# Float32 value products in the sixth to eighth pair of heads, in place of VectorE's low halves

## Chip, cores and metric

The kernel runs on one core of a Trainium2 chip. The metric is the device time of one launch in microseconds (us), the median over several runs. One execution of the same program was recorded by the hardware profiler; every row below is from that execution.

## What is computed

Attention with pooled queries, then a gated feed-forward block, then a soft mixture of experts. Only the attention is touched by the change:

```
q_pool = q.reshape(B, H, S // 2, 2, D).mean(axis=3)          # B=4, H=8, S=1152, D=64
scores = (1 / sqrt(D)) * matmul(q_pool, k.transpose(0, 1, 3, 2))
scores = scores - max(scores, axis=-1)
attn   = exp(scores) / (sum(exp(scores)) + 1e-9)
x      = matmul(attn, v)                                     # -> (2304, 512)
h      = silu(x @ w_gate) * (x @ w_val)                      # d_ff = 1536
y      = h @ w_out ; then dispatch, 8 experts (512 -> 1024 -> 512), combine
```

All inputs and the output are float32.

## The kernel before

**Steps and units.** The attention walks over 16 steps, one for each batch and pair of heads (`steps`, four pairs in each of four batches). A step has 21 units: nine key chunks of 128 for each of the two heads against 512 queries, and three units that hold the remaining 64 queries of both heads (six 64-wide parts each). `unit` computes the scores of one unit on TensorE (L501 and L504, two float16 products with float32 accuracy between them), ScalarE takes the exponential into a float32 tile `P32` (L509), and the weights go to the value product.

**Two ways to the value product.** In the usual way the float32 weights are cut in two: the high half is read in place as bfloat16 (`PH`), and the low half `PL` is a subtraction into float16 (L519), on GpSimd as a rule. `pv` (for the first 512 queries) and `pv_rem` (for the rest) then issue three products for each 128 queries: high weights by high values, high by low, low by high (L546, L550, L551; L538 for the rest). In the other way, the float32 one, no `PL` is made; `pv` issues one float32 product of `P32` with the raw float32 values `vr` (L544; L538 for the rest). `F32_PART` says for which share of a step's units that is done; `share` adds the share up unit by unit and fires when it passes one. Before, it holds for the steps 0 to 4 (counted from zero). `DVE_PART` says in the same way for which share of step 5's units L519 goes to VectorE.

**Who else works in these steps.** In step i the row maxima of step i+1 are made: 18 wide products (L418), each reduced by VectorE (L424), then `nm`, then a copy on ScalarE, then a small DMA into the bias row of `QH` (L444), on which the next step's L504 waits. `split_pair` and `split_high` cut the next pair's keys and queries in halves (casts on ScalarE, subtractions L320 on VectorE and L322, L340 on GpSimd) and copy them by DMAs of the SP queue (L326 to L335). From step 2 to step 8 the gate and value weights are fetched and converted (L697, L708, L712, L714, L771, L772) and kept as halves in six tiles `wgv[0..5]`. From step 4 on, the feed-forward blocks (L807, L811, L812 and `slice_halves`) are worked into the attention by a pace in steps, not in time: one block by step 8, and 4.8 more by step 16.

**Raw values.** `load_pair` loads a pair's keys, queries and values two steps ahead (L216, L219, L223). The raw values `vr` lie in a ring of two places (`VRB = 2`). A place comes free when the pair's cast to high values (L229, ScalarE), its low values (L340, GpSimd) and its last float32 product have read it.

**Order.** The program order is written by the loops at the end of the kernel; a planner with its own timeline of costs then sets the order on each engine and queue. Each engine and each queue runs its own instructions in that order.

Of the kernel before, what the change touches and what calls it, by code (L numbers as in the profile page):

```python
# [11 lines left out]
F32 = mybir.dt.float32  # L12
# [5 lines left out]
ALU = mybir.AluOpType  # L18
# [12 lines left out]
HI_DVE, LO_PART = 0.0, 1.0  # L31
LD0, LDP = 1, 4
Y5E = 2
DVE_PART = [0.0, 0.0, 0.0, 0.0, 0.0, 0.3]
CAST_STEPS = 16
BAR = 2
HIGH0, SPLIT0 = 4, 18
# [16 lines left out]
MOE_PACE = [(4, 0.0), (8, 1.0), (16, 5.8)]  # L54
PREP_BEG, PREP_END = 2, 8
FETCH_LEAD, FETCH_BEG = 2, 0.3
F32_PART = [0.17, 0.0, 0.17, 0.25, 0.33]
VRB = 2
HNB = 1
SUBS = ["al", "l"]  # L60
# [23 lines left out]
def tile_pool_attention_glu_softmoe(  # L84
# [13 lines left out]
    nc = tc.nc  # L98
    B, NP, _, S = kT.shape
    SQ = qT.shape[4]  # L100
    D = 64
    P = 128
    NCH = S // P
# [16 lines left out]
    def ps(tag, shape, dtype=F32, bufs=1, name=None):  # L120
        return psum.tile(shape, dtype, tag=tag, bufs=bufs, name=name or tag)
# [10 lines left out]
    def after(ins, name):  # L132
        dep = mybir.DependencyInfo(mybir.DependencyClass.NoSync, mybir.DependencyReason.SCHED_ONLY)
        tc.add_manual_dep(ins.ins, name, dep, reason="pace")
# [27 lines left out]
    wgv = [wpool.tile([P, 2, 2, ND, SL], F16, tag=f"y{i}", name=f"wgv{i}") for i in range(DFF // SL)]  # L162
# [9 lines left out]
    at = attn_stack.enter_context(tc.tile_pool(name="attn", bufs=1, side="right"))  # L172
# [34 lines left out]
    def load_pair(b, p):  # L207

        r = slice(D if (b, p) == steps[0] else 0, P)
        if (b, p) == steps[1]:  # L210
            kr, qr = (t.rearrange("p a h d n -> p (a h d n)")[:, :2 * S].bitcast(F32) for t in wgv[-4:-2])
            qr = qr.rearrange("p (a q) -> p a q", a=2)
        else:
            kr = at.tile([P, S], F32, tag="kraw", bufs=1, name=f"kr{b}_{p}")
            qr = at.tile([P, 2, SQ], F32, tag="qraw", bufs=1, name=f"qr{b}_{p}")
        k_load = nc.sync.dma_start(out=kr[r], in_=kT[b, p, r])  # L216
        if (b, p) == steps[1]:
            after(k_load, k_first[-1])
        q_load = nc.sync.dma_start(out=qr[r], in_=qT[b, p, r])  # L219
        if (b, p) == steps[1]:  # L220
            after(q_load, k_load.ins.name)
        vr = at.tile([P, 2, NCH, D + 1], F32, tag="vraw", bufs=VRB, name=f"vr{b}_{p}")
        nc.sync.dma_start(out=vr, in_=vP[b, p])  # L223
        raw[b, p] = (kr, qr, vr)

# [251 lines left out]
            next(maxs)  # L477
            n_rm[0] += 1

    n_plain, n_dve, n_hi, n_lo = [0.0], [0.0], [0.0], [0.0]  # L480

    def of_step(parts, i):
        return parts[i] if i < len(parts) else 0.0

    def share(n, part):

        n[0] += part
        if n[0] >= 1.0:
            n[0] -= 1.0
            return True  # L490
        return False

    def unit(b, p, key, parts, n):

        tg, bf = ("mm", MMB) if b * NP + p < ST_STEPS and key % ST_OF == 1 else ("st", STB)
        t = ps(tg, [P, QT], bufs=bf, name=f"st{b}_{p}_{key}")
        o = 0
        for hd, c, q0, w in parts:
            KK, KL, QQ, QH = st[b, p, hd][:4]
            k = slice(c * P, (c + 1) * P)  # L500
            mm = nc.tensor.matmul(t[:, o:o + w], KK[:, k], QQ[:, q0:q0 + w], start=True, stop=False)  # L501
            if (b, p) == steps[0] and 0 < key < NCH:
                after(mm, mx_first[2 * key - 1 if key < ST_LAST else -1])
            nc.tensor.matmul(t[:, o:o + w], KL[:, k], QH[:, q0:q0 + w], start=False, stop=True)  # L504
            o += w

        pl = share(n_plain, of_step(F32_PART, b * NP + p))
        P32 = at.tile([P, QT], F32, tag="P32", bufs=PB, name=f"P32{b}_{p}_{key}")
        ins = nc.scalar.activation(P32[:, :o], t[:, :o], AF.Exp, scale=1.0 / 16.0)  # L509
        if (b, p) == steps[0] and key == EXP_Q:  # L510
            after(ins, highs[steps[1]][-1])
        marks.append(ins.ins.name)
        if pl:
            return P32, None

        PH = P32.bitcast(BF16).rearrange("p (n t) -> p n t", t=2)[:, :, 1]
        PL = at.tile([P, QT], F16, tag="PL", bufs=PB, name=f"PL{b}_{p}_{key}")
        eng = nc.vector if share(n_dve, of_step(DVE_PART, b * NP + p)) else nc.gpsimd
        eng.tensor_tensor(out=PL[:, :o], in0=P32[:, :o], in1=PH[:, :o], op=ALU.subtract)  # L519
        return PH, PL  # L520

    def pv_rem(acc, PH, PL, b, p, parts):
# [42 lines left out]
    def attn(b, p):  # L565
# [82 lines left out]
        for n, parts in enumerate(units):  # L648
            i = b * NP + p
            assert (b, p) in has_max or i == 0  # L650
            maxima(MX0 + MXP * i if i or parts[0][0] or parts[0][2] == QT else 9)
            with tc.high_priority(offset=HP_U0 if b == 0 else HP_U1):
                u = unit(b, p, n, parts, n)
            todo.append((pv_unit, parts, *u))
            yield

            for _ in range(2):
                _, c, q0, _ = todo[0][1][-1]
                if len(todo) <= LAG + (c == 0 and q0 == 0):
                    break  # L660
                pv_next()
                yield
# [407 lines left out]
    with tc.high_priority():  # L1070
        selections()
    first = first_load()
    load_pair(*steps[0])
    split_pair(*steps[0], first)
    if BAR == 1:
        tc.no_sync_barrier()
    load_pair(*steps[1])
    if BAR == 2:
        tc.no_sync_barrier()
# [66 lines left out]
    for i, (b, p) in enumerate(steps):  # L1146
        for u, _ in enumerate(attn(b, p)):
# [3 lines left out]
            f = (u + 1) / UNITS  # L1151
            if i == 0 and u == HIGH0:
                split_high(*steps[1])
            if u == (SPLIT0 if i == 0 else 0):
                if i + 1 < len(steps):
                    split_pair(*steps[i + 1])
                if i + 2 < len(steps):
                    later(0 if i == 0 else LOAD_LAG, lambda k=i + 2: load_pair(*steps[k]))
# [34 lines left out]
    n = NEE  # L1193
# [37 lines left out]
    for c in range(2):  # L1231
        for f in range(NF // 4):
# [6 lines left out]
            out=GT.rearrange("p (f h c) s -> p f h c s", h=2, c=2)[:, :, :, c], in_=gts[c]  # L1239
# [163 lines left out]
    for z, w in enumerate(ZW):  # L1403
        n = HALF // w
        so[z] = so[z]()
        for g in range(NG):
            for c in range(NC2):
                for e in range(NQ):
                    a = NQ * g + e
# [68 lines left out]
```

## Time and profile before

| | |
|---|---|
| Runs | 803.87, 805.23, 808.65 us; median 805.23 |
| Profiled execution | 808.7 us, of it 805.8 us from the first to the last instruction |
| Mean granted TensorE clock | 0.984 of full |
| Busy share of the span | TensorE 95%, its weight loads 72%, VectorE 66%, GpSimd 53%, ScalarE 50% |

A share is an average over stages with different limits. The steps of the attention begin (first exponential of the step) at 15.8, 55.8, 85.7, 115.5, 143.5, 180.5, 217.0, 250.7 and 280.2 us for the steps 0 to 8; steps 8 to 15 end at 630.1 us. The end of a matmul is modelled in such a profile, so what TensorE can issue is read from the distance between starts.

### The profile page before, as it was taken

What the parts mean: (1) busy time and instruction counts of PE and PEld (TensorE: products, weight loads), DVE (VectorE), ACT (ScalarE), POOL (GpSimd) and SP (SyncE); (2) the same over time, 40 slices, a digit from 0 to 9 for tenths busy, and PEclk for the clock granted to TensorE, in tenths of its full rate; (3) what the DMA queues carried; (4) which work ended last, traced back from release to release, by engine and by line L of the source; (5) the groups of instructions that cost most, each with busy time, mean ns of one, the idle gap of its engine ahead of it and who ended that gap; (6) DMA issues with size and microseconds to landing.
All of it is one profiled execution on the core that took longest, in us unless ns stands there. A gap on an engine that the chain in (4) does not pass through costs nothing.

```text
span 805.8 us, 23145 instructions
## 1 busy us (share of the span) xinstructions
PE 765.3 (95%) x9673; PEld 580.1 (72%) x9673; DVE 532.6 (66%) x1059; ACT 399.7 (50%) x770; POOL 423.1 (53%) x396
## 2 busy tenths in 40 slices
PE   5969899999999899999999999999999999999896
PEld 1546567787777677877787878778788988888544
DVE  6677888779997977676768675776552455454323
ACT  4545879777787744444544544444444222122112
POOL 9868877646587943755666666656555100000200
PEclk9989999999999999999999999999999999999898
DMA  8426879949789453533565454414113399368799
GB/s 244 110 79 193 222 202 272 252 159 242 199 253 234 135 110 84 126 98 87 114 138 139 113 116 140 93 28 107 28 24 46 87 313 294 54 184 222 256 410 367
DMA packets 115656, 132.42 MB, mean 164 GB/s; under 512 B 82272, under 2 KB 88352, under 8 KB 111328
## 3 DMA queue, kind: packets, MB, share of 16 engines
q1 hardware_dynamic: 113392, 130.92, 58.9%
q8 instruction: 75, 1.23, 0.7%
q10 hardware_dynamic: 2160, 0.04, 0.1%
q14 instruction: 29, 0.24, 0.1%
HBM read 84.10 MB, written 7.86 MB: 114 GB/s over the span
## 4 chain that ended last, share of the span: by engine, by line
PE 77%; DVE 11%; DMA 6%; ACT 2%; issue 2%; SPq 1%; POOL 0%; DVEq 0%; ACTq 0%; POOLq 0%
PE st L504 7%; PE st L501 7%; PE g L807 6%; PE mx L418 6%; PE g L812 6%; PE g L811 6%; PE v L807 5%; PE v L811 5%; PE v L812 5%; PE pv L550 3%; PE pv L546 3%; PE pv L551 3%; DVE mp L424 3%; PE pv L538 3%; PE hp L1337 2%
## 5 line engine op out<-in xcount | busy, mean ns | idle before, releaser
L519 POOL TENSOR_TENSOR PL<-P 128x512 f16<-128x512 f32 (+1 forms) x311 | 325.5, 1060 | 173.8 <-ACT P L509 170.7
L509 ACT ACTIVATE P<-st 128x512 f32<-128x512 f32 (+1 forms) x336 | 192.9, 582 | 168.0 <-PE st L504 124.8
L424 DVE TENSOR_REDUCE mp<-mx 128x1 f32<-128x512 f32 x270 | 180.1, 683 | 54.7 <-PE mx L418 53.6
L504 PE MATMUL st<-QH,KL 65*128 65x512 f16 (+1 forms) x576 | 148.6, 294 | 9.4 <-DMA QH<-mt 6.1
L501 PE MATMUL st<-QQ,KK 128*128 128x512 f16 (+1 forms) x576 | 147.9, 291 | 1.2 <-ACT P L509 0.9
L546 PE MATMUL pv<-VV,P 128*128 128x65 f16 x1088 | 140.2, 194 | 0.3 <-DVE x L583 0.3
L550 PE MATMUL pv<-VV,P 128*128 128x64 f16 x1088 | 140.0, 196 | 0.0
L551 PE MATMUL pv<-VV,PL 128*128 128x65 f16 x1088 | 138.3, 193 | 0.0
L807 PE MATMUL g<-xT,wgv 128*128 128x256 f16 x432 | 117.7, 273 | 2.1 <-DVE wgv L772 1.5
L546 PEld LDWEIGHTS <-P 128*128 128x128 bf16 x1088 | 104.8, 99 | 18.6 <-issue 3.8
L812 PE MATMUL g<-xT,wgv 128*128 128x256 f16 x432 | 117.8, 273 | 0.0
L811 PE MATMUL g<-xT,wgv 128*128 128x256 f16 x432 | 117.8, 273 | 0.0
L811 PE MATMUL v<-xT,wgv 128*128 128x256 f16 x432 | 117.7, 272 | 0.0
L812 PE MATMUL v<-xT,wgv 128*128 128x256 f16 x432 | 117.6, 272 | 0.0
L807 PE MATMUL v<-xT,wgv 128*128 128x256 f16 x432 | 117.6, 272 | 0.0
L551 PEld LDWEIGHTS <-PL 128*128 128x128 f16 x1088 | 104.6, 100 | 10.3 <-issue 1.1
L550 PEld LDWEIGHTS <-P 128*128 128x128 bf16 x1088 | 104.3, 99 | 8.1 <-issue 0.7
L418 PE MATMUL mx<-kh,QD 128*128 128x512 f16 x270 | 103.5, 395 | 4.2 <-DVE mp L424 2.6
L811 PEld LDWEIGHTS <-wgv 128*128 128x128 f16 x864 | 84.3, 98 | 18.4 <-issue 3.2
L807 PEld LDWEIGHTS <-wgv 128*128 128x128 f16 x864 | 84.4, 98 | 16.0 <-ACT lo L712 1.4
L812 PEld LDWEIGHTS <-wgv 128*128 128x128 f16 x864 | 84.4, 98 | 14.5 <-issue 0.4
L504 PEld LDWEIGHTS <-KL 65*128 65x128 f16 x576 | 53.8, 99 | 32.4 <-issue 13.4
(203 smaller groups left out, 1214.6 us busy)
## 6 DMA issues: line engine op xcount, KB each, us to landing
w<-in_w SPq DMA_DIRECT2D x30, 1024.0 KB, 8.3
vr<-in_vP SPq DMA_DIRECT2D x16, 585.0 KB, 4.9
KK<-kh SPq DMA_DIRECT2D x62, 144.0 KB, 2.7
kr<-in_kT SPq DMA_DIRECT2D x14, 576.0 KB, 4.5
qr<-in_qT SPq DMA_DIRECT2D x14, 576.0 KB, 4.9
r<-in_w_out SPq DMA_DIRECT2D x12, 512.0 KB, 5.0
r<-in_w_gate SPq DMA_DIRECT2D x24, 256.0 KB, 4.4
r<-in_w_val SPq DMA_DIRECT2D x24, 256.0 KB, 4.7
```

The lines of the kernel that those rows point to most:

```text
L418: nc.tensor.matmul(t, q, kh[:, k0:k0 + kw], start=True, stop=True)
L424: ins = nc.vector.reduce_max(out=mp[:, g, c:c + 1], in_=t, axis=AX.X)
L501: mm = nc.tensor.matmul(t[:, o:o + w], KK[:, k], QQ[:, q0:q0 + w], start=True, stop=False)
L504: nc.tensor.matmul(t[:, o:o + w], KL[:, k], QH[:, q0:q0 + w], start=False, stop=True)
L509: ins = nc.scalar.activation(P32[:, :o], t[:, :o], AF.Exp, scale=1.0 / 16.0)
L519: eng.tensor_tensor(out=PL[:, :o], in0=P32[:, :o], in1=PH[:, :o], op=ALU.subtract)
L546: mm = nc.tensor.matmul(dst[:, :D + 1], PH[:, q], VV[:, c, 0, :], start=first, stop=False, skip_group_check=True)
L550: nc.tensor.matmul(dst[:, :D], PH[:, q], VV[:, c, 1, :D], start=False, stop=False, skip_group_check=True)
L551: nc.tensor.matmul(dst[:, :D + 1], PL[:, q], VV[:, c, 0, :], start=False, stop=(c == NCH - 1), skip_group_check=True)
L807: mm = nc.tensor.matmul(o, w[:, 0, d, f], xh, start=(d == 0), stop=False)
L811: nc.tensor.matmul(o, w[:, 0, d, f], xl, start=False, stop=False)
L812: nc.tensor.matmul(o, w[:, 1, d, f], xh, start=False, stop=(d == ND - 1))
```

## The change

`DVE_PART` and its use go: every low half is GpSimd's. `F32_PART` is carried on to the steps 5, 6 and 7 with shares of 0.33, 0.34 and 0.34, in the last two only for the units 0 to 10 (`F32_LAST`). By `share`, these are the units 2, 5, 8, 11, 14, 17, 20 of step 5, the units 2, 5, 8 of step 6 and 0, 2, 5, 8 of step 7: fourteen, of which one (unit 20) is of the kind that holds the remaining queries. The units of the steps 0 to 4 stay as they are. The raw values of the steps 2 and 5 (`VR_W`, the third and sixth pair) are loaded into the last weight place `wgv[-1]`, which also held the first head's keys at the start and gets its weights in the last sixth of the conversion; the ring of two then serves the other pairs.

```diff
-DVE_PART = [0.0, 0.0, 0.0, 0.0, 0.0, 0.3]
-F32_PART = [0.17, 0.0, 0.17, 0.25, 0.33]
+F32_PART = [0.17, 0.0, 0.17, 0.25, 0.33, 0.33, 0.34, 0.34]
+F32_LAST = [99, 99, 99, 99, 99, 99, 11, 11]
+VR_W = (2, 5)
...
-        vr = at.tile([P, 2, NCH, D + 1], F32, tag="vraw", bufs=VRB, name=f"vr{b}_{p}")
+        if b * NP + p in VR_W:
+            vr = wgv[-1].rearrange("p a h d n -> p (a h d n)").bitcast(F32)[:, :2 * NCH * (D + 1)]
+            vr = vr.rearrange("p (h c d) -> p h c d", h=2, c=NCH)
+        else:
+            vr = at.tile([P, 2, NCH, D + 1], F32, tag="vraw", bufs=VRB, name=f"vr{b}_{p}")
...
-        pl = share(n_plain, of_step(F32_PART, b * NP + p))
+        pl = n < of_step(F32_LAST, b * NP + p) and share(n_plain, of_step(F32_PART, b * NP + p))
...
-        eng = nc.vector if share(n_dve, of_step(DVE_PART, b * NP + p)) else nc.gpsimd
-        eng.tensor_tensor(out=PL[:, :o], in0=P32[:, :o], in1=PH[:, :o], op=ALU.subtract)
+        nc.gpsimd.tensor_tensor(out=PL[:, :o], in0=P32[:, :o], in1=PH[:, :o], op=ALU.subtract)
```

## Rows read from the trace of the kernel before

**Rows 1.** Windows: length, busy us (instructions) of PE, PEld, DVE, ACT, POOL, then clock.

```profile
180.50:217.00 36.50, 34.52 (x475) 26.49 (x472) 34.20 (x59) 27.25 (x54) 21.97 (x18) 1.00 0.86 229
217.00:250.70 33.70, 33.48 (x464) 25.52 (x463) 28.48 (x56) 26.95 (x54) 26.75 (x24) 1.00 0.86 232
250.70:280.20 29.50, 27.28 (x367) 19.11 (x365) 27.31 (x50) 24.89 (x50) 27.49 (x24) 0.94 0.61 176
...
376.40:419.10 42.70, 42.70 (x564) 33.96 (x562) 28.92 (x52) 21.28 (x39) 28.13 (x25) 1.00 0.59 129
```

**Rows 2.** Waits of TensorE from 180 to 282 us: total us, times, longest.

```profile
PE g L807 <- DVE wgv L772: 1.5, 1, 1.5
PE st L504 <- DMA QH<-mt: 1.1, 1, 1.1
PE mx L418 <- DVE mp L424: 0.4, 1, 0.4
PE st L501 <- ACT P L509: 0.4, 2, 0.2
```

**Rows 3.** TensorE in order of time: start us, us to the end, what, count.

```profile
172.12 0.19 PE L546 MATMUL pv<-VV,P 128*128 128x65 f16 x1
...
172.87 0.38 PE L501 MATMUL st<-QQ,KK 128*128 128x512 f16 x1
...
176.69 1.08 PE L544 MATMUL pv<-vr,P 128*128 128x65 f32 x8
177.60 0.59 PE L418 MATMUL mx<-kh,QD 128*128 128x512 f16 x2
...
180.78 0.28 PE L538 MATMUL pv<-VV,P 128*128 128x130 f16 x2
...
181.30 0.38 PE L418 MATMUL mx<-kh,QD 128*128 128x512 f16 x1
...
184.44 0.66 PE L538 MATMUL pv<-vr,P 128*128 128x130 f32 x4
184.94 0.38 PE L418 MATMUL mx<-kh,QD 128*128 128x512 f16 x1
```

**Rows 4.** Groups, 180.5 to 280.2 us: count, busy us, mean ns, idle before.

```profile
L519 POOL TENSOR_TENSOR PL<-P 128x512 f16<-128x512 f32 (+1 forms) x57 | 61.4, 1096 | 22.7 <-ACT P L509 21.8 <-DVE W2S L753 0.7
...
L519 DVE TENSOR_TENSOR PL<-P 128x512 f16<-128x512 f32 (+1 forms) x6 | 6.8, 1132 | 0.0
L424 DVE TENSOR_REDUCE mp<-mx 128x1 f32<-128x512 f32 x54 | 35.8, 681 | 4.5 <-PE mx L418 4.4
```

**Rows 5.** In order of time, around TensorE's longest wait of the three steps.

```profile
271.97 2.02 DVE L291 COPY QD<-qh 64x576 f16<-64x576 f16 x2
...
274.76 0.27 PE L807 MATMUL g<-xT,wgv 128*128 128x256 f16 x1 [1.47 <-DVE wgv L772]
```

**Rows 6.** Groups of the whole span: the same copies.

```profile
L291 DVE COPY QD<-qh 64x576 f16<-64x576 f16 x30 | 18.8, 627 | 2.2 <-ACT qh L229 2.0
```

**Rows 7.** Windows of the two half-clock stretches within the attention.

```profile
53.60:63.90 10.30, 7.98 (x42) 3.81 (x43) 8.02 (x8) 5.16 (x10) 8.55 (x7) 0.50 0.48 110
275.50:278.90 3.40, 3.40 (x53) 3.08 (x52) 2.58 (x1) 1.90 (x4) 3.40 (x3) 0.50 0.00 0
```

**Rows 8.** Raw values in order of time: loads of the SP queue, ScalarE's cast.

```profile
37.98 8.82 SPq L223 DMA_DIRECT2D vr<-in_vP  x2
...
190.01 0.87 SPq L223 DMA_DIRECT2D vr<-in_vP  x2
...
224.87 1.11 SPq L223 DMA_DIRECT2D vr<-in_vP  x1
...
252.96 1.19 ACT L229 CAST VV<-vr 128x1170 f16<-128x1170 f32 x1 [0.64 <-PE pv L538]
```

**Rows 9.** DMA issues: count, KB each, median us to landing.

```profile
vr<-in_vP SPq DMA_DIRECT2D x16, 585.0 KB, 4.9
```

**Rows 10.** Waits of TensorE from 0 to 180 us.

```profile
PE st L504 <- DMA QH<-mt: 4.9, 2, 4.6
```

More of the change, by code (lines that the diff above doesn't have):

```diff
@@ L478, in maxima @@
             n_rm[0] += 1
-    n_plain, n_dve, n_hi, n_lo = [0.0], [0.0], [0.0], [0.0]
+    n_plain, n_hi, n_lo = [0.0], [0.0], [0.0]
     def of_step(parts, i):
```

## Prediction

> **What bounds the kernel now.** I read the windows of the steps 5 to 7 first, since all new products fall there. The reader is to see that TensorE is busy 34.52 of 36.5, 33.48 of 33.7 and 27.28 of 29.5 us, and that from step 8 on it has stretches with no idle time at all (42.70 of 42.70) [rows 1]. The work of those later steps is handed out by steps and not by time, so it can't absorb a delay: what the steps 5 to 7 gain or lose on TensorE is carried to the end one for one. In the same three windows VectorE is busy 34.2, 28.5 and 27.3 us and GpSimd 22.0, 26.8 and 27.5 us: three engines are close to full, and TensorE is the fullest in the sum (95.3 of 99.7 us, against 90.0 and 76.2).
>
> Next come TensorE's waits in this stretch. There are few: 1.5 us for the last converted gate weights, 1.1 us for the row maxima of the next step by way of their DMA, 0.4 us for a reduction and 0.4 us for the exponential [rows 2]. None names GpSimd. The clock is the last loss: after the wait of 1.47 us at 274.76 the granted clock is 0.50, the 1.2 GHz level, for 3.4 us [rows 5, 7]. TensorE is busy through all of it, so that costs half of 3.4, 1.7 us.
>
> All that can be won back in the three steps is therefore idle time and clock: (36.5 − 34.52) + (33.7 − 33.48) + (29.5 − 27.28) = 4.4 us, and 1.7 us, together 6.1 us [rows 1, 7]. The idle time is a little understated, because the modelled end of a matmul lies behind the start of the next one: a product that starts every 0.03 us is shown 0.19 us long [rows 3] (0.75 us for 24 between 172.12 and 172.87). With some seven such waits, 0.16 us each, the estimate of what could be won rises by at most 1.1 us, to 7.2 us.
>
> **What it removes on VectorE and GpSimd.** Step 5 loses six low halves of VectorE, 6.8 us in all [rows 4]. GpSimd made 57 low halves in the three steps. It makes 63 − 14 = 49 after the change: 8 fewer, at 1.1 us some 9 us of its 76. Neither stands on TensorE's path by itself: GpSimd's low halves wait 21.8 us for exponentials there, so it has spare time, and VectorE's reductions wait 4.4 us for TensorE [rows 4]. What they are worth is what they take off the 6.1 us.
>
> **What it adds on TensorE.** A float32 unit of the usual kind has four products in eight records. From 176.69 to the next start at 177.60 they take 0.91 us. The float16 way has 12 products; 24 of them take 0.75 us, so 12 take 0.375 us [rows 3]. A unit costs 0.535 us more, and thirteen of them 6.96 us. The fourteenth, with the remaining queries, has six records at (184.94 − 184.44)/4 = 0.125 us, 0.75 us, against nine from 180.78 to 181.30, 0.52 us: 0.23 us more. Sum: **+7.2 us on TensorE**, nothing of which other work can hide, since it is TensorE's own issue time.
>
> The Trainium skill (FP8 and Floating Point Precision, TensorE Precision Notes) says that a true float32 product takes four passes through the array. By that rule, as an estimate, a product would take four times the 0.031 us of a float16 one, a unit 0.5 us, and the fourteen units would add under 2 us in place of 7.2. The trace does not agree for this shape: 0.228 us for one product, over seven times a float16 one; the measured duration stands in the sum.
>
> **Raw values.** The third and sixth pair's values move to the last weight place, and the ring's order shifts. Before, the third and fourth pair's loads are issued at 37.98 to 46.8 us, the second of them after a wait of 8 us [rows 8]; nothing behind them on the queue was ready in that time, so an earlier load there is worth nothing that I can see. The sixth pair's load has to be over before step 5 and its readers before the last sixth of the weight conversion (one sixth of six steps, so step 7): its last product comes with the end of step 5, 217 us, so nothing waits. New waits stand at the places that the seventh and eighth pair leave. The ninth pair's load was one of the two at 190.01; now it has to wait for the last float32 product of step 6, unit 8. With a lag of three units that is about 217.0 + 33.7 × 12/21 = 236 us, and with 4.9 us to land [rows 9] 241 us. Its cast ran at 252.96 [rows 8], so 12 us are left. The tenth pair's load, at 224.87 before, goes to about 250.7 + 29.5 × 12/21 = 268 us, for a cast near 293 us. Both are hidden as long as the planner puts them behind what else the queue has to issue. I cost them at nothing, and at up to 5 us where it does not (rival three). No arithmetic or transfer is added: sixteen value loads before and after.
>
> **What comes back.** Each of the four waits is for VectorE or for work behind it. The row maxima at the end of step 5 follow 18 reductions in a step where VectorE is busy 34.2 of 36.5 us; without 6.8 us of low halves they are early, and TensorE comes later by its own added 3.7 us: 1.1 us gone. The gate weights, read at 274.76, are behind two copies that took 2.02 us [rows 5], where they take 0.627 us each over the whole span [rows 6]. That chain runs from DMA through ScalarE to VectorE and does not read what TensorE adds, and TensorE reaches it later, having four float32 units in step 7 ahead of it; I take the 1.5 us and the 1.7 us of clock as gone. The two small waits make 0.8 us. Together 5.1 of the 6.1 us. Below it the bound is nothing recovered; above, the 7.2 us.
>
> What slowed those copies is beside this sum. GpSimd is busy 27.49 of 29.5 us in that step [rows 1]. The Trainium skill (SBUF — State Buffer, Who interferes with whom) says that VectorE's copies in their fast modes and its two-input operations can be blocked for the whole of a GpSimd instruction, whichever of the two began second. By that rule eight GpSimd instructions fewer give VectorE some time back too; the trace's pair of 2.02 us fits it, and it would not alter a term above, because the wait is already counted as gone.
>
> **Sum.** +7.2 − 5.1 = +2.1 us. The profiled execution took 808.7 us with a span of 805.8; its sum gives 810.8 us. It lies 3.5 us above the median of the runs, 805.2, and the prediction is made on that: 805.2 + 2.1 = **807.3 us**. By the bounds of what comes back the likeliest case alone reaches from 7.2 − 7.2 = 0 to about +4, so 805 to 809 us; the execution-to-execution spread (803.9 to 808.7) is as wide.
>
> **Rivals.** *One, the waits only move (slower).* The reductions read what TensorE writes (4.4 us of waiting for L418 [rows 4]), so a later TensorE makes later maxima: the wait for the row maxima and the one for the weights stand again at the end of each step, and all of the added time shows: +7.2, 812.4 us. For it: VectorE stays over 84% busy in steps 6 and 7, which lose no VectorE work. Against it: the weights' chain does not start from TensorE. It decides if the waits of [rows 2] are still there with 3 us or more.
>
> *Two, VectorE paces these steps (faster).* If VectorE's queue and not TensorE's issue sets the length, TensorE's products are pushed apart by gaps shorter than the modelled tail of a matmul, the float32 products fall into them, and the 6.8 us of low halves come off: 805.2 − 6.8 = 798.4 us. For it: VectorE at 94% in step 5 and 93% in step 7, and the waits name VectorE. Against it: TensorE would need 7.2 + 6.8 = 14 us of gaps, and the rows show 4.4 us idle. It decides if the three steps together come under 96 us from 99.7.
>
> *Three, the new place for the values blocks the queue (slower).* If the planner leaves the ninth pair's load at its place in the program, near 225 us, the SP queue stands until 236 us. Behind it are weight fetches and the transposes of attention outputs; the fetches run two conversions ahead, 36 conversions in six steps of 33 us each, so some 11 us are covered, as much as the wait. What is left I set at 5 us at most: 812 us.
>
> *Four, the order changes elsewhere (faster).* A re-planned order can remove the wait of 4.6 us [rows 10] at the end of step 0 and the 10.3 us at half clock after it, in which TensorE is busy 7.98 us [rows 7]: 4.6 + 4 = 8.6 us, then 805.2 + 2.1 − 8.6 = 798.7 us. For it: the third pair's values can come 20 us earlier. Against it: that wait ends with the row-maximum chain of VectorE, which reads no values.
>
> **How the numbers follow.** The forecast has 0.46, rival one 0.22, rival two 0.16, rival three 0.08, rival four 0.08. A change within 0.5% (4 us) is about what can't be told from none here. The forecast lies within it, the rivals one and three above, two and four below: faster 0.24, same 0.46, slower 0.30. A range from 798.5 to 812.5 us holds the forecast and reaches to the slower rivals' times and to the faster ones', with about half of each of those on its edges left out.
>
> **What would show it.** Right: L544 has 128 + 104 = 232 records, and L538's float32 records 24; a unit's eight records take 0.91 us; L519 on VectorE is gone and on GpSimd has 303 in place of 311; the three windows together grow by 1 to 4 us, with TensorE's idle time under 1.5 us and no half-clock stretch near 275 us; the later steps keep their lengths. Wrong: the windows shrink (rival two), the waits return (rival one), the SP queue stands at a value load in step 6 or 7 (rival three), or the difference lies before 180 or after 330 us, where the change has no work (rival four, and any other effect of the planner's order).

## The result and the profile after

The changed kernel takes 811.47 us (median of 18 runs, 805.45 to 815.05), the kernel before 806.77 us (18 runs beside them, 803.87 to 811.02). The ratio is 1.0054, with a 95% interval of 1.0036 to 1.0073: slower by 0.54%, some 4.4 us. The forecast was 807.3 us on a median of 805.2, so +2.1 us; the range of 798.5 to 812.5 us holds the time. The profiled execution of the changed kernel took 809.54 us with a span of 807.7; that of before took 808.7 with 805.8. The two profiles are thus 1.9 us of span apart, and what they show is the smaller part of the difference; the rest is taken up at the end of this document.

Lines 501 to 551 of before are 506 to 555 here (L504 is L509, L519 is L523, L544 is L548, L538 is L542, L807 is L811, L772 is L776). First the page of the changed kernel, and its groups of float32 products by shape:

```profile
span 807.7 us, 23014 instructions
PE 771.2 (95%) x9618; PEld 587.5 (73%) x9618; DVE 523.6 (65%) x1053; ACT 398.7 (49%) x770; POOL 413.4 (51%) x388
L523 POOL TENSOR_TENSOR PL<-P 128x512 f16<-128x512 f32 (+1 forms) x303 | 315.5, 1053 | 188.4 <-ACT P L514 185.9
...
L548 PE MATMUL pv<-vr,P 128*128 128x65 f32 x160 | 22.5, 273 | 0.0
...
L548 PE MATMUL pv<-wgv,P 128*128 128x65 f32 x72 | 9.9, 276 | 0.0
L542 PE MATMUL pv<-wgv,P 128*128 128x130 f32 x12 | 1.7, 278 | 0.0
L542 PE MATMUL pv<-vr,P 128*128 128x130 f32 x12 | 1.7, 278 | 0.0
```

The change does what its text says: 303 low halves, all on GpSimd, 160 + 72 = 232 float32 records of the usual kind and 24 of the kind with the remaining queries. The records that read `wgv` are the third and sixth pair's, out of the last weight place.

A step is counted here from its first exponential to the next step's. The windows of the changed kernel, steps 3 to 8, and then steps 5 to 8 as one:

```profile
114.90:144.10 29.20, 27.04 (x356) 20.57 (x355) 22.88 (x46) 24.57 (x50) 20.79 (x19) 1.00 0.84 248
144.10:182.20 38.10, 38.06 (x428) 29.00 (x427) 27.91 (x55) 27.43 (x53) 19.59 (x18) 0.96 0.69 194
182.20:216.90 34.70, 34.60 (x418) 27.39 (x414) 29.15 (x55) 26.18 (x53) 19.35 (x17) 1.00 0.83 199
216.90:249.40 32.50, 32.30 (x426) 25.42 (x423) 25.60 (x51) 26.59 (x54) 20.98 (x19) 1.00 0.83 223
249.40:282.50 33.10, 32.18 (x415) 24.29 (x413) 28.47 (x52) 26.02 (x52) 22.89 (x22) 1.00 0.68 196
282.50:333.00 50.50, 50.50 (x642) 39.80 (x639) 33.52 (x71) 21.92 (x42) 30.23 (x26) 1.00 0.50 110
...
182.20:333.00 150.80, 149.58 (x1890) 116.90 (x1886) 116.74 (x226) 100.71 (x199) 93.46 (x82) 1.00 0.69 173
```

The same stretches of the kernel before, where they were not shown yet:

```profile
115.50:143.50 28.00, 27.32 (x353) 20.11 (x352) 23.18 (x47) 25.13 (x50) 19.91 (x18) 1.00 0.84 245
143.50:180.50 37.00, 36.46 (x428) 28.44 (x427) 28.29 (x55) 27.31 (x54) 21.12 (x19) 1.00 0.75 211
...
180.50:331.60 151.10, 145.78 (x1952) 111.14 (x1949) 124.97 (x232) 101.28 (x200) 102.58 (x90) 0.99 0.68 177
```

Two things are to be seen. In steps 5 to 7, where all the new products are, 99.7 us [rows 1] became 34.7 + 32.5 + 33.1 = 100.3 us, and with step 8, into which some work moved, 151.1 became 150.8: there the change costs nothing. TensorE's idle time fell from 151.10 − 145.78 = 5.3 us to 1.2 us, and the granted clock is 1.00 throughout; the half-clock stretch near 275 us [rows 7] is gone. The loss of these two profiles is in the steps 3 and 4, which the change's arithmetic does not touch: 28.0 to 29.2 us and 37.0 to 38.1 us. From step 9 to step 15 every step has the length of before, to 0.1 us.

TensorE's waits between 182 and 283 us in the changed kernel (total us, times, longest) show what became of the four that the forecast named [rows 2]:

```profile
PE g L811 <- DVE W2S L757: 0.4, 1, 0.4
PE g L816 <- DVE wgv L776: 0.2, 1, 0.2
PE st L506 <- ACT P L514: 0.2, 1, 0.2
PE w2p L749 <- ACT r L743: 0.2, 1, 0.2
```

The wait for the gate weights went from 1.5 to 0.2 us, the 1.1 us for the row maxima and the 0.4 us for the reduction are gone.

**Where steps 3 and 4 lose.** Apart from the value loads, every engine and the SP queue have the same order in both kernels until about 116 us. The loads part earlier. The third pair's goes out at 17.61 us (37.98 before), so the ring's second turn serves the fourth and fifth pair, and the fifth pair's load is at 46.07 us in the changed kernel and at 116.98 before. The sixth pair's, into the same weight place as the third's, is at 124.51 us (144.38 before). The first instruction that stands elsewhere is the fifth pair's cast on ScalarE, whose values are now there early. That cast, and what the planner then does with the SP queue around the end of step 3, is in these lists (start us, us, what). The changed kernel:

```profile
116.38 1.19 ACT L234 CAST VV<-vr 128x1170 f16<-128x1170 f32 x1
...
130.15 0.33 SPq L220 DMA_DIRECT2D qr<-in_qT  x1
130.53 0.42 SPq L739 DMA_DIRECT2D wo_d<-r  x1
136.99 0.33 SPq L701 DMA_DIRECT2D r<-in_w_gate  x1
...
140.08 0.47 SPq L336 DMA_DIRECT2D QQ<-qh  x1
```

The kernel before:

```profile
121.90 1.20 ACT L229 CAST VV<-vr 128x1170 f16<-128x1170 f32 x1
...
131.01 0.33 SPq L735 DMA_DIRECT2D wo_d<-r  x1
131.68 0.33 SPq L219 DMA_DIRECT2D qr<-in_qT  x1
135.39 0.33 SPq L697 DMA_DIRECT2D r<-in_w_gate  x1
...
141.25 0.47 SPq L331 DMA_DIRECT2D QQ<-qh  x1
```

The load of the raw queries now stands ahead of a store (`wo_d`), and the weight fetches behind that store wait 6.0 us for it instead of 3.3 us. These are the queue's own waits (total us, times, longest), first of the changed kernel, then of before:

```profile
SPq L701 <- DMA wo_d<-r: 6.0, 1, 6.0
...
SPq L697 <- DMA wo_d<-r: 3.3, 1, 3.3
```

So the four fetches (the first of them is in the lists) go out 1.6 us later, and the copies into `QQ` and `KK` start 1.2 us earlier. Between them falls the transfer that carries the row maxima of step 4 into `QH`, 2.2 KB on ScalarE's queue. It was issued at 139.51 us in the changed kernel and at 140.22 before, 24.6 and 24.7 us after the start of step 3. The windows of its flight and TensorE's first product that needs it, in the changed kernel:

```profile
139.50:143.70 4.20, 2.04 (x35) 1.79 (x32) 0.69 (x1) 2.07 (x4) 2.98 (x3) 1.00 0.85 239
...
143.71 0.38 PE L509 MATMUL st<-QH,KL 65*128 65x512 f16 x1 [2.16 <-DMA KK<-kh]
...
145.20:148.60 3.40, 3.40 (x11) 1.57 (x10) 2.26 (x4) 2.24 (x6) 2.15 (x3) 0.50 0.77 169
```

and in the kernel before:

```profile
140.20:143.10 2.90, 2.55 (x55) 2.07 (x52) 1.49 (x4) 2.36 (x4) 1.93 (x2) 1.00 0.21 48
...
143.13 0.38 PE L504 MATMUL st<-QH,KL 65*128 65x512 f16 x1 [0.38 <-DMA QH<-mt]
```

The last two numbers of a window are the DMA engines' busy share and GB/s. The small transfer flew in 2.9 us while the engines were 21% busy, and took 4.2 us while they were 85% busy. (The wait is put down to `KK<-kh`, but by its issue and its 4.15 us the small transfer landed at 143.66 us, 0.05 us before the product.) TensorE waits 2.16 us in place of 0.38: the transfer takes 1.28 us longer, and in the new order TensorE has half a us less of other work in that time (2.04 us busy against 2.55). Step 3 grows by 1.2 us, as the transfer does. 1.5 us after the wait TensorE's granted clock falls to 0.50, the 1.2 GHz level, for 3.4 us in which it is busy all the time: 1.7 us more.

### The profile page after: what moved, and what is told of

It is laid out like the page before. It is cut to its first block, busy times and chain, and to the rows that moved or that the text cites. A ratio compares the mean times of both kernels' runs of the same rounds, so it can differ in the third digit from the quotient of the medians.

```text
span 807.7 us, 23014 instructions
## 1 busy us (share of the span) xinstructions
PE 771.2 (95%) x9618; PEld 587.5 (73%) x9618; DVE 523.6 (65%) x1053; ACT 398.7 (49%) x770; POOL 413.4 (51%) x388
## 4 chain that ended last, share of the span: by engine, by line
PE 84%; DVE 7%; DMA 3%; ACT 2%; issue 2%; SPq 1%; POOL 0%; ACTq 0%; DVEq 0%; POOLq 0%
PE st L509 8%; PE st L506 7%; PE mx L423 7%; PE g L811 6%; PE g L816 6%; PE v L811 6%; PE g L815 6%; PE v L815 6%; PE v L816 6%; PE pv L554 3%; PE pv L550 3%; PE pv L555 3%; PE pv L542 3%; PE pv L548 3%; PE so4p L1414 2%
## 5 line engine op out<-in xcount | busy, mean ns | idle before, releaser
L523 POOL TENSOR_TENSOR PL<-P 128x512 f16<-128x512 f32 (+1 forms) x303 | 315.5, 1053 | 188.4 <-ACT P L514 185.9
L429 DVE TENSOR_REDUCE mp<-mx 128x1 f32<-128x512 f32 x270 | 180.5, 683 | 58.5 <-PE mx L423 56.8
L509 PE MATMUL st<-QH,KL 65*128 65x512 f16 (+1 forms) x576 | 146.8, 294 | 9.9 <-DMA QH<-mt 4.5
L506 PE MATMUL st<-QQ,KK 128*128 128x512 f16 (+1 forms) x576 | 145.6, 291 | 0.7 <-ACT P L514 0.7
L550 PE MATMUL pv<-VV,P 128*128 128x65 f16 x1036 | 133.3, 194 | 0.3 <-DVE x L587 0.3
L554 PE MATMUL pv<-VV,P 128*128 128x64 f16 x1036 | 133.6, 196 | 0.0
L555 PE MATMUL pv<-VV,PL 128*128 128x65 f16 x1036 | 131.0, 193 | 0.0
L811 PE MATMUL g<-xT,wgv 128*128 128x256 f16 x432 | 117.6, 272 | 0.5 <-DVE W2S L757 0.4
L811 PE MATMUL v<-xT,wgv 128*128 128x256 f16 x432 | 117.6, 272 | 0.0
L550 PEld LDWEIGHTS <-P 128*128 128x128 bf16 x1036 | 100.1, 99 | 16.7 <-issue 3.1
L555 PEld LDWEIGHTS <-PL 128*128 128x128 f16 x1036 | 99.3, 100 | 8.8 <-issue 0.6
L554 PEld LDWEIGHTS <-P 128*128 128x128 bf16 x1036 | 99.0, 98 | 8.9 <-issue 0.7
L811 PEld LDWEIGHTS <-wgv 128*128 128x128 f16 x864 | 84.6, 98 | 14.7 <-issue 1.0
L509 PEld LDWEIGHTS <-KL 65*128 65x128 f16 x576 | 52.6, 99 | 31.4 <-issue 12.3
```

The source lines that it names most:

```text
L429: ins = nc.vector.reduce_max(out=mp[:, g, c:c + 1], in_=t, axis=AX.X)
L523: nc.gpsimd.tensor_tensor(out=PL[:, :o], in0=P32[:, :o], in1=PH[:, :o], op=ALU.subtract)
L550: mm = nc.tensor.matmul(dst[:, :D + 1], PH[:, q], VV[:, c, 0, :], start=first, stop=False, skip_group_check=True)
L554: nc.tensor.matmul(dst[:, :D], PH[:, q], VV[:, c, 1, :D], start=False, stop=False, skip_group_check=True)
L555: nc.tensor.matmul(dst[:, :D + 1], PL[:, q], VV[:, c, 0, :], start=False, stop=(c == NCH - 1), skip_group_check=True)
L811: mm = nc.tensor.matmul(o, w[:, 0, d, f], xh, start=(d == 0), stop=False)
```

## The experiments

The theories: A, the placement of the third pair's values re-orders the steps 3 and 4, and that is the loss; B, the float32 products are the loss, since TensorE has no room for them. "Steps" are compared by their starts in the profile, and "before" is the kernel before, run on the same chip beside each.

**1. The placement alone** (e1_place_only), on the kernel before:

```diff
+VR_W = (2, 5)
...
-        vr = at.tile([P, 2, NCH, D + 1], F32, tag="vraw", bufs=VRB, name=f"vr{b}_{p}")
+        if b * NP + p in VR_W:
+            vr = wgv[-1].rearrange("p a h d n -> p (a h d n)").bitcast(F32)[:, :2 * NCH * (D + 1)]
...
+        else:
+            vr = at.tile([P, 2, NCH, D + 1], F32, tag="vraw", bufs=VRB, name=f"vr{b}_{p}")
```

> The kernel before with only the new place for the raw values of the third and sixth pair; the float32 units and VectorE's low halves stay as before. Theory A (the loss sits in steps 3 and 4, made by the changed order around the fifth and sixth pair's value loads and the half-clock stretch behind it): +2 to +4 us, with a wait of some 2 us before the first L504 of step 4 and a half-clock stretch near 145 us. Rival B (the loss is the float32 products' own issue time, the placement is free): 0 us, within 1 us, and step 4 starts at 143.5 us as before.

Measured 808.12 us against 807.43, ratio 1.0015 (0.9995 to 1.0034): too wide to settle anything. Its steps say more. Steps 3 and 4 are 1.5 us longer than before (66.5 against 65.0 us): the row maxima's transfer takes 3.68 us, TensorE waits 1.69 us, and no half-clock stretch follows in that profile. But steps 5 to 8 are shorter by 3.1 us (148.0 against 151.1). So the placement does two things of opposite sign, and the forecast had put both at nothing.

**2. The float32 products with all values in the ring** (e2_f32_ring), the changed kernel with

```diff
-VR_W = (2, 5)
+VR_W = ()
```

> The changed kernel with every pair's raw values in the ring of two, so the float32 products of steps 5 to 7 alone. Theory A: within 2 us of before, since the 7.2 us of products are paid for by waits and half clock that go in steps 5 to 8; steps 3 and 4 as before. Rival B: +4 to +7 us, about as the full change. Theory C (the ring blocks the queue): over +7 us, with the SP queue standing at a value load in step 5 or 6.

Measured 811.63 us, ratio 1.0053 (1.0031 to 1.0075): as slow as the changed kernel, which at the time spoke for B. The profile says that it is another loss. Steps 3 and 4 run as before (the transfer in 2.9 us, a wait of 0.37 us), and steps 5 to 8 grow:

```profile
180.50:335.10 154.60, 150.51 (x1897) 117.76 (x1894) 119.44 (x226) 101.55 (x199) 93.16 (x82) 1.00 0.69 177
...
217.10:253.70 36.60, 33.38 (x432) 25.71 (x430) 28.17 (x53) 26.51 (x52) 23.27 (x21) 1.00 0.89 225
...
225.69 1.19 ACT L234 CAST VV<-vr 128x1170 f16<-128x1170 f32 x1 [2.19 <-DMA vr<-in_vP]
227.42 0.38 PE L506 MATMUL st<-QQ,KK 128*128 128x512 f16 x1 [0.86 <-ACT P L514]
```

With two places only, each held until its pair's last float32 product, a load goes out at 221.00 us and ScalarE stands 2.19 us before its cast; the exponentials behind the cast are late for TensorE. The sixth pair's place is what prevents this in the changed kernel.

**3. All low halves on GpSimd, nothing else** (e3_gpsimd_low), on the kernel before:

```diff
-DVE_PART = [0.0, 0.0, 0.0, 0.0, 0.0, 0.3]
+DVE_PART = []
```

> The kernel before with VectorE's six low halves of step 5 given to GpSimd, no float32 unit added, values in the ring. It tells what VectorE's relief is worth without TensorE's added time. If VectorE paces step 5 (rival two of the prediction): -3 to -7 us. If TensorE paces it: -2 to 0 us, with the wait for the row maxima at the end of step 5 (1.1 us) gone.

Measured 809.01 us, ratio 1.0012 (0.9988 to 1.0037). Step 5 is 2.6 us shorter, but steps 5 to 8 together only 1.0 us (150.1 against 151.1). VectorE's 6.8 us do not set the time of these steps.

**4 and 5. Both kernels again.** The changed kernel once more (e4_changed_again), with its times, and one profile of the kernel before (e5_before_profile); neither has an edit.

> The changed kernel once more on the same chip as the three others, for its profile, its spread and the clock of each run. +4 to +5 us by the runs so far. If the spread comes from half-clock stretches, span times mean clock is the same within 1.5 us in runs that differ by 5 us or more.

> The kernel before, unchanged, for a second profile. Theory D (the credit for waits and clock in the prediction was partly luck of one execution): the wait for the gate weights near 273 us or the half-clock stretch behind it is absent, and the steps 5 to 8 together are 1 to 3 us shorter than the 151.1 us of the first profile. Rival E (they belong to the kernel): both are there again and the steps 5 to 8 take 151 us within 0.5.

The changed kernel: 810.84 us, ratio 1.0039 (1.0016 to 1.0063); its steps 3 and 4 are 2.1 and 1.1 us longer than before, with the small transfer at 5.02 us, a wait of 3.03 us and a half-clock stretch at 147.3 us. Span times clock lies between 793.7 and 796.3 us over its twelve runs, not within the 1.5 us that were expected, so the spread is not clock alone. The kernel before took 811.13 us in that one execution; its steps 5 to 8 took 151.0 us and had the wait of 1.5 us for the weights and the 3.4 us at half clock again, so these belong to the kernel and not to one execution. It also shows how one execution may mislead: its step 3 was 31.0 us long by a half-clock stretch at 116.5 us that the other profiles of this kernel have not.

**6, 7 and 8. The price of the products, elsewhere and doubled.** Fourteen float32 units in the steps 9 and 10 of the kernel before (e6_f32_late); 29 in place of 14 in the changed kernel (e7_f32_double); and seven units in step 1, the kernel before with the placement of experiment 1 (e8_f32_step1):

```diff
-F32_PART = [0.17, 0.0, 0.17, 0.25, 0.33]
+F32_PART = [0.17, 0.0, 0.17, 0.25, 0.33, 0.0, 0.0, 0.0, 0.0, 0.33, 0.34]
```

```diff
-F32_PART = [0.17, 0.0, 0.17, 0.25, 0.33, 0.33, 0.34, 0.34]
+F32_PART = [0.17, 0.0, 0.17, 0.25, 0.33, 0.66, 0.68, 0.68]
```

```diff
-F32_PART = [0.17, 0.0, 0.17, 0.25, 0.33]
+F32_PART = [0.17, 0.33, 0.17, 0.25, 0.33]
+VR_W = (2, 5)
```

> The kernel before with fourteen more float32 units in steps 9 and 10 (twelve usual, two of the remaining queries) in place of none in steps 5 to 7; VectorE's low halves of step 5 stay. There TensorE has almost no wait to give back, so the run prices the units themselves: 12 x 0.535 + 2 x 0.23 = +6.9 us if the price per unit is right, all of it within steps 9 and 10. Under +4 us would mean the price is too high; over +9 us, that a wait is added.

> The changed kernel with float32 shares 0.66, 0.68, 0.68 in steps 5 to 7: 29 units in place of 14. If what could be won back is used up by the first fourteen, the fifteen more add their whole price, 14 x 0.535 + 0.23 = +7.7 us over the changed kernel, +12 us over before. If GpSimd's or VectorE's relief still pays (rival two of the prediction), the step from 14 to 29 is under +4 us.

> The kernel before with the new place for values and seven float32 units in step 1 (none there before), none added in steps 5 to 7. Step 1 has 8.5 us in which TensorE issues nothing or runs at half clock, so the added 6 x 0.535 + 0.23 = 3.4 us may be hidden: 0 to +1 us over the placement alone if so, and below before if GpSimd's seven instructions less take off a wait of ScalarE there (1.6 us at 63 us). +3 to +4 us if the step's length is set by TensorE's issue after all.

The late units: 810.38 us, ratio 1.0060 (1.0038 to 1.0082), +4.8 us where +6.9 was expected. In the profile step 9 grows by only 0.8 us, from 44.8 to 45.6, since it had 1.9 us of idle time to give (TensorE busy for 42.86 us before, 45.53 here). Step 10, with none before (42.70 of 42.70 [rows 1]), is the clean price:

```profile
379.80:425.60 45.80, 45.80 (x540) 37.35 (x539) 29.01 (x52) 21.35 (x39) 19.41 (x17) 1.00 0.58 138
```

45.8 − 42.7 = 3.1 us for seven units. Six of them are of the usual kind and one holds remaining queries, which the forecast would price at 6 × 0.535 + 0.23 = 3.4 us, a tenth too much. The distances between starts show where the tenth lies. A float16 value product takes 0.0313 us to TensorE's next start, as a mean over the steps 9 and 10 of the kernel before, and twelve take 0.376 us, as the forecast had it. A float32 record takes 0.1077 us over the same steps here, and the eight of a unit 0.86 us, where the forecast had 0.91 from a single unit. A usual unit thus costs 0.486 us, and 6 × 0.486 + 0.23 = 3.1 us. The doubled units: 817.77 us, ratio 1.0142 (1.0110 to 1.0174). Against the changed kernel that is 0.0088 of 806.8, 7.1 us, by the first comparison, and 8.3 us by that of experiment 4, for fifteen units, as expected (+7.7). In its profile steps 5 to 8 have

```profile
184.70:341.70 157.00, 155.93 (x1831) 124.74 (x1829) 119.41 (x226) 101.99 (x200) 77.77 (x67) 1.00 0.70 166
```

6.2 us more than the changed kernel (150.8): with the idle time used up, the fifteen units cost near their full price (14 × 0.486 + 0.23 = 7.0 us). The units in step 1: 812.9 us, ratio 1.0087 (1.0059 to 1.0115), and step 1 is 4.3 us longer for seven units; the ratio lies 0.0072, 5.8 us, above that of the placement alone, so the units were not hidden. The profile has a half-clock stretch of 13.7 us at 52.9, longer than the 10.3 of before [rows 7], and two of 3.4 us at 90.5 and 121.2; so this run prices the products at another clock and doesn't tell A from B.

**9 and 10. The third pair back in the ring**, the sixth still placed: the changed kernel (e9_one_place), and the kernel before with that one placement alone (e10_one_place_only, the lines of experiment 1 with the tuple shown here):

```diff
-VR_W = (2, 5)
+VR_W = (5,)
```

```diff
+VR_W = (5,)
```

> The changed kernel with only the sixth pair's values in the weight place (the third pair's in the ring), so that the planned order up to the middle of step 4 is that of the kernel before, and the fourteen float32 units stay. Theory A (placing the third pair's values re-orders steps 3 and 4, which opens the wait of 2.2 us before step 4 and the half-clock stretch near 145 us): both are gone, steps 3 and 4 are 65 us as before instead of 67.4, and the time is +0 to +2.5 us over before. Rival B (the float32 units are the loss wherever the values lie): +4 to +6 us, no matter that the wait is gone.

> The same with no float32 units added in steps 5 to 7 and VectorE's low halves kept: the sixth pair's values moved, nothing else. Both theories: within 1.5 us of before. The run before this one less this one is the price of the fourteen units with VectorE's relief: 0 to +2.5 us by theory A, +4 us or more by rival B.

Experiment 9 decides between A and B. It has all fourteen float32 units and the low halves of the change, and takes 807.56 us against 808.31, ratio 0.9985 (0.9963 to 1.0006): the loss is gone, and its interval lies under the changed kernel's. Its profile has the small transfer in a quiet stretch again:

```profile
120.30:148.40 28.10, 27.36 (x353) 20.16 (x352) 23.27 (x48) 25.12 (x50) 19.99 (x18) 1.00 0.85 242
...
145.00:148.00 3.00, 2.56 (x55) 2.08 (x52) 1.59 (x4) 2.41 (x5) 2.02 (x2) 1.00 0.21 46
...
148.00 0.38 PE L509 MATMUL st<-QH,KL 65*128 65x512 f16 x1 [0.44 <-DMA QH<-mt]
...
185.10:336.00 150.90, 149.38 (x1888) 116.84 (x1886) 115.80 (x226) 100.91 (x200) 93.58 (x82) 1.00 0.67 175
```

Step 3 has 28.1 us, the DMA engines are 21% busy in the transfer's flight, the wait is 0.44 us, and no half-clock stretch follows; steps 5 to 8 are those of the changed kernel (150.9). Apart from the value loads its orders are those of the kernel before up to what stands there at 147 us. The sixth pair's load moves in it too, to 18.15 us, where the changed kernel has it at 124.51, and this early load costs nothing in steps 3 and 4. (The spans of the two profiles are alike, 807.7 and 807.4 us, since that of experiment 9 has two half-clock stretches of 3.4 us, at 78.1 and 88.3 us; the loss shows in the medians.) Experiment 10 takes 806.30 us, 1.3 us less than experiment 9, ratio 0.9985 (0.9961 to 1.0009), with steps 5 to 8 of

```profile
180.10:328.90 148.80, 144.22 (x1944) 110.44 (x1942) 123.94 (x232) 100.69 (x200) 102.86 (x90) 1.00 0.68 177
```

so the sixth pair's place by itself takes 2.3 us off these steps, with the half-clock stretch near 275 us gone, and no float32 product has any part in that. Neither version can be told from the kernel before.

**11 and 12. One more profile of each kernel** (e11_changed_profile, e12_before_profile), without an edit, for the steps 3 and 4:

> The changed kernel, a third profile. Theory A: the wait before step 4 of 2 to 3 us and the half-clock stretch near 146 us are there a third time, and steps 5 to 8 together take 151 us within 0.5, as in the first two.

> The kernel before, a third profile. Theory A: no wait over 1 us and no half-clock stretch between 140 and 150 us, steps 5 to 8 in 151 us with the half-clock stretch after the wait for the gate weights near 275 us or, without it, 149.4 us.

The changed kernel (810.32 us) waits 3.25 us and has 3.4 us at half clock from 145.7 us on; the kernel before (805.70 us) waits 0.37 us and has none there.

```profile
140.00:145.20 5.20, 1.99 (x33) 1.73 (x30) 0.69 (x1) 2.01 (x4) 3.63 (x3) 1.00 0.86 236
...
145.24 0.38 PE L509 MATMUL st<-QH,KL 65*128 65x512 f16 x1 [3.25 <-DMA QH<-mt]
```

The profiles of this place together. In the first two rows the four fetches go out between 19.8 and 21.2 us after the start of step 3, in the rows below between 21.5 and 23.7 us:

| kernel (number of the experiment) | third pair placed | DMA busy in its flight | transfer, us | TensorE's wait, us | half clock after it |
|---|---|---|---|---|---|
| before; 12 | no | 0.21; 0.20 | 2.87; 2.86 | 0.38; 0.37 | none |
| one place, 9; alone, 10 | no | 0.21; 0.20 | 2.93; 2.86 | 0.44; 0.37 | none |
| placement alone, 1 | yes | 0.61 | 3.68 | 1.69 | none |
| changed; 4; 11 | yes | 0.85; 0.88; 0.86 | 4.15; 5.02; 5.24 | 2.16; 3.03; 3.25 | 3.4 us each |
| doubled, 7 | yes | 0.86 | 4.31 | 2.32 | 3.4 us |
| units in step 1, 8 | yes | 0.26 | 3.6 | 1.11 | none |

In the five profiles of the third and fourth of these rows and of the doubled units, step 3 is longer than the 28.0 us of before by 0.7 to 2.3 us, in each by what its transfer takes more, within 0.1 us. The trace of the DMA packets shows how the transfer grows. It has 144 packets (queue q10; count, MB, share of 16 engines), and before they all lie within 0.2 us, here in 141.3 to 141.6 us. In the changed kernel 135 lie in 141.0 to 142.2 us among 223 packets of the SP queue, none in 142.2 to 142.9, and the last nine, a sixteenth, in 142.9 to 143.1:

```profile
q10 hardware_dynamic: 144, 0.00, 26.1%
...
q10 hardware_dynamic: 135, 0.00, 6.2%
...
q10 hardware_dynamic: 9, 0.00, 2.5%
```

In experiment 8, whose DMA share does not fit, the last nine start at 149.36 us, 1.2 us after the others, as a single packet of 16 KB on another queue (148.18 to 149.38 us) ends.

## Why the prediction was right in part, and where it failed

**The time.** It lies in the range, and the side that had 0.46, no difference beyond 0.5%, was missed by little: 0.54% slower. The forecast named +2.1 us for the float32 products and what comes back. The three steps that it was made for grew by 0.6 us, under the 1 to 4 us that were its sign of being right, and by −0.3 us with step 8. The loss of +4.4 us lies elsewhere, so that the sum came near the measured time is in part luck.

**The float32 products, +7.2 us: a little too large.** By the distances between starts in experiment 6 a usual unit costs 0.486 us and not 0.535, and the fourteen 13 × 0.486 + 0.23 = 6.5 us. The term that was mis-sized is the float32 unit, read off one unit as 0.91 us where the mean is 0.86; the 0.375 us of the float16 way were right. Steps 5 to 8 of experiments 9 and 10 differ by the products and the low halves alone, and there TensorE's busy time rises by 149.38 − 144.22 = 5.2 us only. Busy time counts the modelled ends, so gaps shorter than such an end count as busy; that the other 1.3 us lie there is near the 1.1 us that the forecast allowed for them, and is not shown. The Trainium skill (FP8 and Floating Point Precision, TensorE Precision Notes) counts four passes for a float32 product, which by the estimate in the forecast made a unit 0.125 us dearer; the 0.486 us measured do not agree.

**What comes back, 5.1 us: right in kind, and not from where I said.** In steps 5 to 7 TensorE's idle time fell from 4.4 to 1.2 us and the 1.7 us of clock came back, 4.9 of the 6.1 us (5.8 us with step 8). But part of that is the sixth pair's place. Steps 5 to 8, in us, by what is done; the three profiles of the kernel before lie within 151.0 to 151.2, those of the changed kernel within 150.8 to 150.9, the others are one profile each:

| | low halves as before, no new products | changed low halves, fourteen new units |
|---|---|---|
| no value in the weight place | 151.1 (before) | 154.6 (experiment 2) |
| sixth pair there | 148.8 (10) | 150.9 (9) |
| third and sixth pair there | 148.0 (1) | 150.8 (changed) |

Read across, products and low halves together cost 2.1 us with the sixth pair placed, 2.8 with both and 3.5 with none: the forecast's +2.1 was about right as a sum, with both its terms some 0.7 us too large (of 6.5 us, 4.4 come back; by busy time, 3.1 of 5.2). Read down, the sixth pair's place gives 2.3 to 3.7 us, and so pays for them.

**The raw values, "I cost them at nothing": this step failed, twice.** The new place of the sixth pair is worth those 2.3 to 3.7 us, and the third pair's earlier load, "worth nothing that I can see", costs 1.5 us in experiment 1 and 2.3, 3.3 and 3.4 us in the three profiles of the changed kernel, all in steps 3 and 4 and against the 65.0 us of the first profile of before (65.3 in its third). I had looked for who waits for the load, and found nobody. What it does is to change the place of other work in the planned order, 70 us later: first a cast, then DMAs. That the third pair's place is the cause of this loss in steps 3 and 4, and that without it the loss in time is gone, is shown by experiment 9; not all of the 4.4 us is found in these two steps (below). That the small transfer is slowed by the fetches and copies in flight is read from the table's DMA shares and from its packets, which lie among theirs; the fetches by themselves were not moved, so that link is argued and not shown.

**The rivals.** One, the waits only move: the four waits are gone, and steps 5 to 8 did not grow. Two, VectorE paces: the three steps together did not come under 96 us, and experiment 3 gives the relief alone 1.0 us. Three, the value load blocks the SP queue: the ninth pair's load went out at 238.32 us and its cast ran at 259.95, a cover of over 15 us; it did not happen. Four, the order changes elsewhere: that is the mechanism that decided, at another place and with the opposite sign. The half clock after step 0, which it was to remove, is still there (from 53.0 us). I had named "any other effect of the planner's order" as what would make the forecast wrong, with a difference before 180 us as its mark, and had given it no price: that is the step of the prediction that failed.

**What stays open.** From the profiles, steps 3 to 8 explain 2.3 − 0.3 = +2.0 us in one profile of the changed kernel and +3.1 in the other two, of +4.4 by the first comparison and +3.1 by the second (experiment 4); that fits within the intervals of 1.5 to 1.9 us each way. But the kinds do not fit. In experiment 4, where both kernels ran on one chip, span times clock, the work at full clock, is 0.6 us higher for the changed kernel (794.6 against 794.0), and the time lost to the clock is 3.0 us higher (14.3 against 11.3), while in steps 3 to 8 the stretch at 145 us has only taken the place of the one at 275 us. The profiles show one more place. A half-clock stretch near 750 us, 6.8 to 10.3 us long, stands in all three profiles of the changed kernel and in one of three of before. The part after step 15, in which it lies, takes 175.2 to 176.1 us in the changed kernel; before, it takes 175.7 us with the stretch and 173.2 and 172.7 without. Experiment 9 has no such stretch. First the changed kernel, then experiment 9:

```profile
631.60:807.70 176.10, 165.60 (x1929) 127.50 (x1926) 77.26 (x203) 38.66 (x80) 6.15 (x17) 0.96 0.77 250
...
634.50:807.40 172.90, 161.60 (x1931) 124.40 (x1927) 77.35 (x203) 38.75 (x81) 6.18 (x17) 0.98 0.79 255
```

So a part of what experiment 9 wins over the changed kernel, some 3 us by these two profiles, may lie there. What brings that stretch about is not shown; it also stands in experiment 10, which has the third pair in the ring and is not slower than before. Nor is it shown why the planned order of steps 5 to 8 is better with the sixth pair placed, beyond the half-clock stretch near 275 us that is absent there.

## What to carry to other kernels

A load that is moved to an earlier time can change everything that a planner places after it: find the first place where the two planned orders part, and read what stands there, before the move is costed at nothing. Price added TensorE work against the idle time and the half-clock time of its own steps: the first fourteen units cost 2 to 3.5 us net in their steps, the next fifteen 6.2 us, near their full price of 7.0. And of a tiny transfer on the path between two steps, ask which large ones are in flight beside it.

## What the runs showed of the hardware that was not expected

A transfer of 2.2 KB took 2.9 us with the DMA engines 20% busy and 3.7 to 5.2 us with them 61 to 88% busy, and 3.6 us in one profile where they were 26% busy; its 144 packets lay within 0.2 us in the table's first two rows and over 1.4 to 2.5 us in the others. After waits of TensorE of 2.2 to 3.3 us at the start of step 4 the granted clock fell to the 1.2 GHz level for 3.4 us in all four profiles that have such a wait; after those of 1.7 and 1.1 us there it did not, though it did after the 1.47 us at 274.76 of the kernel before [rows 5, 7]. Where it fell, the wait cost 1.7 us beyond its own length. And the spread of one kernel's times is largely clock: between the shortest and the longest of the changed kernel's 18 runs, 803.7 us of span at a mean clock of 0.990 and 813.3 us at 0.978, the span grows by 9.6 us and the time lost to the clock (span times one less the clock) by 9.9 us; a straight line through all 18 gives 0.77 us lost for each us of span.
